# First chunk's v loaded as fp32 and cast on the engines, two of its loads moved behind weight pieces, first expert steps moved ahead

## Chip, cores and metric

The kernel runs on one core of a Trainium2 chip. The metric is the device time in microseconds (us) of one execution; the smaller, the better. Compute engines named below are PE (matrix multiply), DVE (vector), ACT (activation) and POOL (GpSimd); SP issues most transfers, POOL issues the others. All transfers share 16 DMA engines.

## What is computed

Two stages in a row. The first is a gated linear recurrence for 4 batches and 8 heads over 768 steps, with head size 48:

```python
f = 1.0 / (1.0 + np.exp(-f_logit))
for t in range(S):
    state = f[:, :, t, :, None] * state + np.einsum('bhd,bhe->bhde', k[:, :, t], v[:, :, t])
    y[:, :, t] = np.einsum('bhd,bhde->bhe', q[:, :, t], state)
```

The second takes the 3072 rows of 384 that come out and sums four expert networks, weighted by normalised probabilities:

```python
p = domain_probs / (domain_probs.sum(-1, keepdims=True) + 1e-09)
for e in range(E):                       # 4 experts, 384 -> 1024 -> 384
    out += p[:, e:e + 1] * (np.maximum(x @ w1[e], 0.0) @ w2[e])
```

## The kernel before

**Tiling.** The 768 steps are cut into six chunks of 128 (`c` = 0 to 5). Inside a chunk, each batch `b` has its recurrence turned into matrix products: `cs` and `cq` (L351, L362) sum the log gates on PE, `exps` and `expq` (L382, L387) turn the sums into factors on ACT, `q` and `k` (L394, L397) multiply q and k by the factors on DVE or POOL, `tpq` and `tpk` (L406) transpose the products on PE, `ev_tp` (L288) copies them out of PSUM, `at` (L437) makes the 128 x 128 scores, `ev_at0` and `ev_at1` (L449 on DVE, L445 on ACT) copy the two halves out, where the copy on ACT is masked afterwards by `mask1` on POOL (L441), and `y` (L464) multiplies them with `vb`, the bf16 values. `ev_y` copies y out, `xt` transposes it (L490) and `ev_xt` puts it where the experts read it. `kv` (L470) and `ev_kv` (L477) add the chunk to the carried state.

**Experts.** In chunk 0 the first expert's first layer goes batch by batch, in eight steps `h 0.0.fc.n` of 12 matmuls each (L499): `fc` 0 or 4 names the half of the hidden columns, `n` = 0, 128, 256, 384 the batch. From the second expert on a step `h` takes all four batches at once (3 matmuls of 512 columns), and steps `o` (L514) and `p` (L646, L654) make the second layer. `pp` (L324) transposes the probabilities.

**Names.** A number pair behind a step is chunk and batch: `y 0.1` is y of chunk 0, batch 1.

**Order.** A planner makes a list of steps with dependencies and a rank for each, taken in turn from the string `RANKS` at the top of the file. Every engine issues its steps in the order of these ranks, so an engine waits at its first step that isn't ready, and all that is behind waits with it. A letter behind a rank fixes the engine of the step: A is ACT, D is DVE, P is POOL. `FILLER` names steps in front of which PE runs matmuls of 512 columns whose result nobody reads (L1156).

**Transfers around the change.** SP issues the loads of f, k and q of chunk 0, then the probabilities. POOL issues, in the order of `SEQ` (L1170), the four loads of chunk 0's v and the eleven pieces of the weights, all on one queue. A transfer issued by POOL casts: the weights go from fp32 to bf16 on the way, and so do chunk 0's four v loads (L293), straight into the tiles `vb`. `w0` and `w1` are the two halves of expert 0's first layer. The first two v loads are held until the loads of k of batches 1 and 2 have landed (`GATE`). For later chunks v is loaded as fp32 by SP and cast by `cast_v` (L402).

**What follows chunk 0's loads.** f of chunk 1 comes in two halves. The second half (`ld f1.1`) is issued only once weight piece 8 has landed (L307). Its gate steps on ACT (L334, L342) stand in front of `cs 1.0` (L347), the first PE step of chunk 1's recurrence.

Of the kernel before, what the change touches and what calls it, by code (L numbers as in the profile page):

```python
# [77 lines left out]
FILLER = {"cs 0.0": 6, "tpk 0.1": 4}  # L78
# [65 lines left out]
def kernel(  # L144
# [11 lines left out]
    nc = tc.nc  # L156
# [1048 lines left out]
```

## Time and profile before

| what | us |
|---|---|
| median of 3 runs | 286.28 |
| the three runs | 286.17, 286.28, 289.65 |
| profiled execution, its time | 285.82 |
| profiled execution, span of its instructions | 284.1 |
| DVE, ACT, POOL busy | 208.7, 178.2, 185.3 |

The profile page lists for each engine its busy time and share of the span. PE is busy nearly throughout, and the others have a quarter to a third of the span free. An answer of the trace with a time line has the start, the length, the engine, the line of the code, what is written and read, and the count of instructions, with the engine's idle time before them and what ended it in brackets.

### The profile page before, as it was taken

What the parts mean: (1) busy time and instruction counts of PE and PEld (TensorE: products, weight loads), DVE (VectorE), ACT (ScalarE), POOL (GpSimd) and SP (SyncE); (2) the same over time, 40 slices, a digit from 0 to 9 for tenths busy, and PEclk for the clock granted to TensorE, in tenths of its full rate; (3) what the DMA queues carried; (4) which work ended last, traced back from release to release, by engine and by line L of the source; (5) the groups of instructions that cost most, each with busy time, mean ns of one, the idle gap of its engine ahead of it and who ended that gap; (6) DMA issues with size and microseconds to landing.
All of it is one profiled execution on the core that took longest, in us unless ns stands there. A gap on an engine that the chain in (4) does not pass through costs nothing.

```text
span 284.1 us, 8015 instructions
## 1 busy us (share of the span) xinstructions
PE 276.0 (97%) x3228; PEld 241.2 (85%) x3228; DVE 208.7 (73%) x437; ACT 178.2 (63%) x350; POOL 185.3 (65%) x197
## 2 busy tenths in 40 slices
PE   6889999999999999999999999999999999999995
PEld 4678565668788999999998999999999899999995
DVE  5695487797779587769887786686765687857683
ACT  5668235647898848686866867769367456556420
POOL 5799353706699878667729955695656545793761
PEclk9999999999999999999999999999999999999999
DMA  6999999999988999999999999996547015201003
GB/s 156 189 195 205 208 195 200 184 216 181 162 150 159 198 164 208 204 168 184 194 175 207 194 179 218 184 166 124 111 82 160 30 31 76 67 0 59 2 2 111
DMA packets 153688, 41.88 MB, mean 147 GB/s; under 512 B 144028, under 2 KB 152860, under 8 KB 153652
## 3 DMA queue, kind: packets, MB, share of 16 engines
q1 hardware_dynamic: 142404, 34.66, 65.1%
q0 software_dynamic: 11248, 6.72, 16.8%
q8 instruction: 25, 0.41, 0.6%
q14 instruction: 11, 0.09, 0.1%
HBM read 31.51 MB, written 4.72 MB: 128 GB/s over the span
## 4 chain that ended last, share of the span: by engine, by line
PE 84%; DMA 9%; POOL 4%; ACT 1%; DVE 1%; issue 0%; ACTq 0%; POOLq 0%
PE ps_m L646 29%; PE ps_m L531 26%; PE ps_m L574 7%; DMA w_sb<-in_moe_w_dram 7%; PE ps_m L514 6%; PE ps_m L499 4%; PE ps_m L654 2%; DMA f<-in_f_logit_dram 2%; PE ps_m L437 2%; POOL w_sb L312 2%; PE ps_m L464 1%; PE ps_m L460 1%; PE ps_m L347 1%; PE ps_m L470 1%; POOL AT L441 1%; PE ps_m L362 1%
## 5 line engine op out<-in xcount | busy, mean ns | idle before, releaser
L531 PE MATMUL ps_m<-x,w_sb 128*128 128x256 bf16 x672 | 84.3, 273 | 0.0
L531 PEld LDWEIGHTS <-w_sb 128*128 128x128 bf16 x672 | 63.6, 98 | 7.1
L595 ACT ACTIVATE h<-ps_m 128x512 bf16<-128x512 f32 x82 | 46.8, 600 | 24.1 <-PE ps_m L531 23.9
L646 PEld LDWEIGHTS <-S 128*128 128x128 bf16 x576 | 48.2, 98 | 0.8
L673 DVE TENSOR_TENSOR o<-ps_m,o 128x192 f32<-128x192 f32 x91 | 31.1, 353 | 19.1 <-PE ps_m L646 17.3
L646 PEld LDWEIGHTS <-h 128*128 128x128 bf16 x432 | 36.2, 98 | 0.8
L610 POOL TENSOR_TENSOR S<-h 128x1024 bf16<-128x1024 bf16 x14 | 29.7, 2124 | 10.3 <-DVE S L610 6.3
L499 PE MATMUL ps_m<-x,w_sb 128*128 128x128 bf16 (+2 forms) x264 | 35.1, 282 | 0.0
L420 ACT ACTIVATE yb<-ps_m,pn 128x384 bf16<-128x384 f32 x55 | 29.4, 586 | 8.5 <-PE ps_m L464 5.6
L397 POOL TENSOR_TENSOR qk<-q,e 128x384 bf16<-128x384 f32 x18 | 21.6, 1201 | 12.5 <-DVE f L549 3.9
L646 PE MATMUL ps_m<-ts_sb,S 128*128 128x192 bf16 x288 | 29.3, 246 | 0.0
L646 PE MATMUL ps_m<-w_sb,h 128*128 128x192 bf16 x288 | 29.2, 246 | 0.0
L646 PE MATMUL ps_m<-w_sb,S 128*128 128x192 bf16 x288 | 28.7, 246 | 0.0
L499 PEld LDWEIGHTS <-w_sb 128*128 128x128 bf16 x264 | 21.6, 98 | 8.1
L593 DVE TENSOR_SCALAR h<-ps_m 128x512 bf16<-128x512 f32 x30 | 20.6, 688 | 9.6 <-PE ps_m L531 8.5
L453 DVE TENSOR_TENSOR AT<-ps_m,mask 128x512 bf16<-128x512 f32 x40 | 25.6, 682 | 2.1 <-PE ps_m L437 2.0
L510 ACT ACTIVATE h<-ps_m 128x512 bf16<-128x512 f32 x33 | 19.1, 595 | 12.2 <-PE ps_m L499 11.8
L380 ACT ACTIVATE e<-ps_m 128x384 f32<-128x384 f32 x40 | 23.6, 708 | 3.2 <-PE ps_m L347 1.4
L610 POOL TENSOR_TENSOR S<-h,S 128x1024 bf16<-128x1024 bf16 x10 | 21.2, 2124 | 4.5 <-DVE o L673 2.5
L514 PE MATMUL ps_m<-w_sb,h 128*128 128x384 bf16 x128 | 23.9, 326 | 0.0
L585 DVE CUSTOM_DVE_ANT_0 h<-ps_m,QK 128x512 bf16<-128x512 f32 x24 | 16.0, 686 | 5.1 <-PE ps_m L574 1.9
L588 ACT COPY QK<-ps_m 128x512 f32<-128x512 f32 x24 | 13.8, 588 | 8.1 <-PE ps_m L574 5.2
(140 smaller groups left out, 523.3 us busy)
## 6 DMA issues: line engine op xcount, KB each, us to landing
out_dram<-o SPq DMA_DIRECT2D x23, 192.0 KB, 2.5
w_sb<-in_moe_w_dram POOLq DMA_DIRECT2D x5, 768.0 KB, 15.2
k<-in_k_dram SPq DMA_DIRECT2D x10, 384.0 KB, 5.1
q<-in_q_dram SPq DMA_DIRECT2D x10, 384.0 KB, 5.0
v<-in_v_dram SPq DMA_DIRECT2D x10, 384.0 KB, 5.1
f<-in_f_logit_dram SPq DMA_DIRECT2D x9, 384.0 KB, 5.8
w_sb<-in_moe_w_dram POOLq DMA_DIRECT2D x6, 384.0 KB, 8.2
f<-in_f_logit_dram SPq DMA_DIRECT2D x6, 192.0 KB, 4.4
```

Of the source, the lines that this page charges most:

```text
L380: nc.scalar.activation(out=o, in_=i, func=AF.Exp, scale=1.0 if j else -1.0)
L397: return engines[eng].tensor_tensor(out=tl("qk", c, b)[:, j, :, 0:D].rearrange("t (i r) d -> t i r d", r=2), in0=tl("qk"[j], c, b // 2)[:, ...
L420: nc.scalar.activation(out=ys, in_=y, func=AF.Copy, scale=pe)
L453: nc.vector.tensor_tensor(out=tl("AT", c, b)[:, r].rearrange("s i t -> s (i t)"), in0=tl("A", c, b, r).rearrange("s i t -> s (i t)"), in1= ...
L499: nc.tensor.matmul(out=hp(c, e, fc, n0, n1, nf)[:, f], lhsT=w1_sb[:, e, kk, (fc + f) * 128:(fc + f + 1) * 128], rhs=tl("xT", c)[:, kk, n0: ...
L514: nc.tensor.matmul(out=tl("op", c, e, nt)[:, 0:Din], lhsT=tl("h", c, e, half_of(c, nt * T))[:, fc, nt * T:(nt + 1) * T], rhs=w2_sb[:, e, f ...
L531: nc.tensor.matmul(out=out_[:, f], lhsT=w1_sb[:, e, kk, (fc + f) * 128:(fc + f + 1) * 128], rhs=tl("xs", c, hf, p)[:, el, kk, :], start=(k ...
L593: nc.vector.tensor_relu(out=dst, in_=tl("hp", c, hf, p, el, fc))
L595: nc.scalar.activation(out=dst, in_=tl("hp", c, hf, p, el, fc), func=AF.Relu)
L610: return engines[eng].tensor_tensor(out=o, in0=in0, in1=in1, op=op)
L646: nc.tensor.matmul(out=out_, lhsT=lhs[:, f, :], rhs=rhs[:, f, :], start=(first and el == 0 and f == 0), stop=(el == 1 and f == KH - 1), sk ...
L673: nc.vector.tensor_tensor(out=o, in0=src, in1=o, op=ALU.add)
```

## The change

Chunk 0's four v loads no longer cast. They go as fp32 into the tiles `v`, as in the later chunks, and a step `v 0.b` casts each into `vb`: `v 0.0` on DVE, `v 0.1`, `v 0.2` and `v 0.3` on ACT. In POOL's queue the third v load comes behind weight piece 0, the fourth behind weight piece 1. The ranks are new, and two fillers are added.

```diff
-FILLER = {"cs 0.0": 6, "tpk 0.1": 4}
+FILLER = {"cs 0.0": 6, "tpk 0.1": 4, "at 0.2": 2, "h 0.0.0.0": 3}
...
         if (c, nm) == (0, "v"):
-            ins[c, nm, b] = nc.gpsimd.dma_start(out=tl("vb", c, b), in_=srcs[nm][c, :, b * H:(b + n) * H, :])
+            ins[c, nm, b] = nc.gpsimd.dma_start(out=tl("v", c, b // 2)[:, hh(b, n), :], in_=srcs[nm][c, :, b * H:(b + n) * H, :])
...
             issued.append(P.add(f"v issue {i}", {"POOL": 0.8}, lambda _, i=i: load(0, "v", i, 1), -600 + 2 * j,
-                                deps=issued[-1:] + gate(x), takes=[("vb", 0, i)], lag=1.2))
-            ld[0, "v", i] = P.add(f"ld v0.{i}", {"DMA": 1.45}, lambda _: None, VW[0] + j, deps=issued[-1:] + fifo[-1:], lag=2.0)
+                                deps=issued[-1:] + gate(x), takes=[("v", 0, i // 2)], lag=1.2))
+            ld[0, "v", i] = P.add(f"ld v0.{i}", {"DMA": 1.0}, lambda _: None, VW[0] + j, deps=issued[-1:] + fifo[-1:], lag=2.0)
...
-            vb = ld[0, "v", b] if c == 0 else P.add(f"v {c}.{b}", {"POOL": 0.52, "ACT": 0.54}, one(cast_v), s(4),
+            vb = P.add(f"v {c}.{b}", {"POOL": 0.52, "ACT": 0.54} if c else {"POOL": 0.52, "ACT": 0.54, "DVE": 0.34}, one(cast_v), s(4),
                        deps=[ld[c, "v", b]], takes=[("vb", c, b)], frees=[("v", c, half)])
...
-SEQ = "v0 v1 v2 w0 v3 w1"
+SEQ = "v0 v1 w0 v2 w1 v3"
```

The new ranks (both strings are left out) leave the order of each engine as it was, but for these places, all in the first tenth of the program:

| engine | order before | order after |
|---|---|---|
| PE | at 0.2, xt 0.0, y 0.1, tpk 0.3, tpq 0.3, pp, kv 0.1, h 0.0.0.0, xt 0.1, at 0.3, y 0.2, kv 0.2, h 0.0.0.128, xt 0.2, h 0.0.4.0, y 0.3, h 0.0.4.128 | 2 fillers, at 0.2, xt 0.0, y 0.1, tpk 0.3, 3 fillers, h 0.0.0.0, tpq 0.3, xt 0.1, kv 0.1, pp, h 0.0.0.128, at 0.3, y 0.2, kv 0.2, h 0.0.4.0, xt 0.2, h 0.0.4.128, y 0.3 |
| DVE | ev_at1 0.0, ev_at0 0.1, ev_tp 0.2, k 0.3, q 0.3, ev_kv 0.0, ev_at0 0.2, ev_tp 0.3, ev_kv 0.1, ev_xt 0.1 | ev_at1 0.0, v 0.0, ev_at0 0.1, ev_tp 0.2, k 0.3, ev_kv 0.0, ev_at0 0.2, q 0.3, ev_xt 0.1, ev_tp 0.3, ev_kv 0.1 |
| ACT | ev_y 0.0, ev_at1 0.2, ev_xt 0.0, ev_y 0.1, ev_tp 0.3, relu 0.0.0.0, ev_y 0.2, relu 0.0.0.128, ev_xt 0.2 | ev_y 0.0, v 0.1, ev_at1 0.2, ev_xt 0.0, ev_y 0.1, ev_tp 0.3, v 0.2, relu 0.0.0.0, ev_y 0.2, v 0.3, relu 0.0.0.128, ev_xt 0.2 |
| POOL | issue of v0, v1, v2, w0, v3, then k 0.2, issue of w1, w2, then mask1 0.1, issue of w3, w4, w5, then mask1 0.2 | issue of v0, v1, w0, v2, then k 0.2, issue of w1, then mask1 0.1, issue of v3, w2, w3, w4, then mask1 0.2, issue of w5 |
| SP | loads of f0.3, k0.3, q0.3, then the probabilities | the probabilities, then f0.3, k0.3, q0.3 |

122 rows, old and new, of the table RANKS are left out of this document.

## The prediction

> **What bounds the kernel now.** I read the page first, then what PE waited for after its first expert step, then the chain that ended last.
>
> ```profile
> span 284.1 us, 8015 instructions
> PE 276.0 (97%) x3228; PEld 241.2 (85%) x3228; DVE 208.7 (73%) x437; ACT 178.2 (63%) x350; POOL 185.3 (65%) x197
> ```
>
> ```profile
> PE ps_m L347 <- ACT gp L342: 0.7, 1, 0.7
> ```
>
> The second fence is the whole answer for PE's waits from 18.9 us to the end: one. From there on PE works without a break, but for that wait at `cs 1.0`. So the change, which lies ahead of 26 us, can act in two ways only: through the time at which PE has got through the start, and through the time at which this one wait ends. The time line of PE around the wait, and the chain that leads to it:
>
> ```profile
> 47.51 0.81 PE L499 MATMUL ps_m<-x,w_sb 128*128 128x512 bf16 x3
> 49.01 0.48 PE L347 MATMUL ps_m<-gp,Ub 128*128 128x384 bf16 x2 [0.68 <-ACT gp L342]
> ```
>
> ```profile
> 22.65 18.79 DMA w_sb<-in_moe_w_dram
> 41.45 5.70 DMA f<-in_f_logit_dram
> 47.24 0.85 ACT f L334
> 48.11 0.85 ACT gp L342
> ...
> 50.81 1.94 PE ps_m L499 x9
> ```
>
> `cs 1.0` waits for the gate steps, these for `ld f1.1`, this for weight piece 8, and that for everything ahead of it in POOL's queue, the four v loads among it. PE's step before it began at 47.51 and holds PE for 0.65 (three matmuls of 512 columns; the last row has nine of them in 1.94), so PE was ready at 48.16 and started at 49.01: **0.85 us of slack**. Call D the delay of PE's stream at that place and X the time by which weight piece 8 lands earlier. Then `cs 1.0` starts at the later of 48.16 + D and 49.01 - X, and since PE doesn't wait afterwards, the whole time moves by the larger of D - 0.85 and -X. A start that costs PE nothing is worth 0.85 us at most.
>
> **X: the loads.** Bytes read stay, bytes written double, the cast goes. The DMA view for 10.5 to 14 us (both queues at work), and for 48 to 51 us, where SP's fp32 loads run alone in rows of 192 bytes, as v will be:
>
> ```profile
> q0 software_dynamic: 1754, 0.17, 91.2%
> q1 hardware_dynamic: 1464, 0.35, 67.3%
> ```
>
> ```profile
> q1 hardware_dynamic: 3620, 0.69, 115.6%
> ```
>
> Columns are packets, MB, and packet time as a share of 16 engines. A cast packet took 0.912 x 3.5 x 16 / 1754 = 29.1 ns, an fp32 packet 1.156 x 3 x 16 / 3620 = 15.3 ns. Packets overlap, so I go by the pace: q0's share of the packet time is 91.2 / 158.5, hence 2.01 us for 1754 packets, 1.18 us for the 1024 of one v load; alone, fp32 makes 1024 in 3 x 1024 / 3620 = 0.85 us. Four loads save 4 x 0.33 = **1.3 us**. The upper bound is by packet times, 4 x 1024 x (29.1 - 15.3) / 16 = 3.5 us; the lower is nothing, if POOL's queue moves an fp32 row no faster, or if the late issue of the fourth load leaves the queue empty for a moment. I take 1.3, the nearest row for the new shape; all that matters is whether it is over 0.6 (below).
>
> The Trainium skill, "DMA: Bandwidth & Descriptors", Specifications, speaks against it: transfers under 512 B are not at line rate because the engine reads, modifies and writes. Both shapes are under 512 B, so by that rule alone X could be 0 and the sum would be 286.3. The two packet times above differ, so I follow the rows.
>
> **D: the start of PE's stream.** PE, POOL, DVE and ACT before:
>
> ```profile
> 15.97 0.40 PE L437 MATMUL ps_m<-QK 48*128 48x128 bf16 x8 [0.53 <-DVE QK L288]
> 16.30 0.34 PE L490 MATMUL ps_m<-ident,yb 128*128 128x128 bf16 x3
> 16.48 0.19 PE L464 MATMUL ps_m<-vb,AT 128*128 128x48 bf16 x1
> 17.39 0.35 PE L464 MATMUL ps_m<-vb,AT 128*128 128x48 bf16 x7 [0.72 <-POOL AT L441]
> 17.58 0.61 PE L406 MATMUL ps_m<-ident,qk 128*128 128x128 bf16 x8
> 18.12 0.66 PE L324 MATMUL ps_m<-ident,o 24*128 24x24 f32 x4
> 18.71 0.34 PE L470 MATMUL ps_m<-vb,qk 128*128 128x96 bf16 x4
> 18.89 0.83 PE L499 MATMUL ps_m<-x,w_sb 128*128 128x128 bf16 x12
> ```
>
> ```profile
> 13.97 1.57 POOL L312 DMA_DIRECT2D w_sb<-in_moe_w_dram  x2
> 15.55 1.78 POOL L441 TENSOR_SCALAR_AFFINE_SELECT AT<-AT 128x512 bf16<-128x512 bf16 x1
> 19.60 0.65 POOL L441 TENSOR_SCALAR_AFFINE_SELECT AT<-AT 128x512 bf16<-128x512 bf16 x1
> ```
>
> ```profile
> 15.24 0.67 DVE L288 COPY QK<-ps_m 112x1024 bf16<-112x1024 bf16 x1
> 15.83 0.55 DVE L397 TENSOR_TENSOR qk<-k,e 128x384 bf16<-128x384 f32 x1
> 16.29 0.56 DVE L394 TENSOR_TENSOR qk<-q,e 128x384 bf16<-128x384 f32 x1
> 19.93 0.36 DVE L288 COPY x<-ps_m 128x384 bf16<-128x384 bf16 x1
> ```
>
> ```profile
> 13.99 0.75 ACT L445 CAST AT<-ps_m 128x512 bf16<-128x512 f32 x1
> 15.38 0.52 ACT L287 CAST yb<-ps_m 128x384 bf16<-128x384 f32 x1
> 16.44 0.73 ACT L445 CAST AT<-ps_m 128x512 bf16<-128x512 f32 x1 [0.54 <-PE ps_m L437]
> 17.03 0.48 ACT L287 COPY x<-ps_m 128x384 bf16<-128x384 bf16 x1
> 19.76 0.60 ACT L510 ACTIVATE h<-ps_m 128x512 bf16<-128x512 f32 x1 [0.49 <-PE ps_m L499]
> ```
>
> ```profile
> 10.05 1.11 SPq L320 DMA_DIRECT2D o<-in_moe_domain_probs_dram  x1
> ```
>
> PE lost 0.53 at `at 0.2`, waiting for DVE's `ev_tp 0.2`, and 0.72 inside `y 0.1`, waiting for `mask1 0.1` on POOL.
>
> *Cast of v 0.0 on DVE.* It stands in front of `ev_tp 0.2`, and DVE has no idle time there. No row has this cast on DVE. The nearest, by size and output, is the copy of 384 elements, 0.36; the fp32 product of the same size, 0.56, is the ceiling; the floor is half the copy, 0.18. I take 0.35. `at 0.2` moves from 15.97 to 16.32. The 2 fillers run in that wait (2 x 0.22, now 0.53 + 0.35 long): nothing. Without the wait they would cost 0.43.
>
> *Mask.* `mask1 0.1` comes one issue earlier. POOL is free of w1 at 13.97 + 1.57 / 2 = 14.75, and the half that it masks is copied by ACT until 13.99 + 0.75 = 14.74. On SP the probabilities, 1.11 to issue, now stand ahead of f0.3. What of that shows in f0.3's landing, no row tells; with all of it `ev_tp 0.2` would be 0.4 later still, with none nothing. I take half, which delays this copy to 15.3 and nothing else. The mask took 1.78 once and 0.65 once; the long one ran beside the two DVE products at 15.83 and 16.29, whose 0.55 + 0.56 is just the excess of 1.13. In the new order those come after 16.1 (`k 0.3`) and after 17.5 (`q 0.3`), so I take 0.65: done at 16.0, with 1.78 at 17.1. The Trainium skill has the mechanism, "GPSIMD Engine Reference", Key points: GpSimd shares its SBUF interfaces with VectorE and contends with instructions there that have two SBUF inputs. The two rows agree. By the rule `y 0.1` no longer waits for the mask; if the rule were not the cause, the mask would end at 17.1, `y 0.1` would be 0.2 later and the sum 285.9.
>
> *y 0.1 and the cast v 0.1.* `at 0.2` 16.32, `xt 0.0` 0.33 later at 16.65, `y 0.1` at 16.83 if `vb` is there. v1 was issued and landed so:
>
> ```profile
> L293 POOL DMA_DIRECT2D vb<-in_v_dram x1: 897/897/897, 8.9 to 8.9; - x1
> DMA to landing us min/median/max: 7.4/7.4/7.4
> ```
>
> It landed at 16.3. Unchanged, ACT casts it from 16.35 to 16.9 (0.52, as `ev_y 0.0`, the cast of the same size), in the 0.54 that ACT idled ahead of `ev_at1 0.2`. So `y 0.1` starts at 16.9, takes 0.19 (17.39 to 17.58), `tpk 0.3` some 0.25 (eight transposes had 0.54): PE is through at 17.34. The 3 fillers last 3 x 0.215 = 0.65, to 17.99.
>
> *h 0.0.0.0* needs `ev_xt 0.0`: `ev_at1 0.2` follows `at 0.2` at 16.78, `ev_xt 0.0` 0.59 later at 17.37, done at 17.85. And it needs w0, which was issued behind v2 and landed so:
>
> ```profile
> L312 POOL DMA_DIRECT2D w_sb<-in_moe_w_dram x1: 768/768/768, 10.7 to 10.7; - x1
> DMA to landing us min/median/max: 8.0/8.0/8.0
> ```
>
> That is 18.7; now v2 with 0.85 or more is behind it: 17.8 or earlier. So the step starts at 17.99, right behind the fillers, which are hidden but for 0.1; if `ev_xt 0.0` were early, all 0.65 would be PE's. Before, it started at 18.89, with `tpq 0.3`, `pp` and `kv 0.1` done, which PE now has still ahead: 0.27 (the other half of the 0.54), 0.59 (18.12 to 18.71) and 0.18 (18.71 to 18.89), together 1.04. D is 17.99 + 1.04 - 18.89 = **+0.14**.
>
> *Rest.* `v 0.2` falls into ACT's idle 0.49 ahead of the first relu (19.76). `v 0.3` stands ahead of `ev_xt 0.2`, which lets `h 0.0.0.256` in: between 0 and its 0.52; I take 0.1, as PE has `h 0.0.4.128` and `y 0.3` to do meanwhile. w1, moved ahead of v3, lands earlier than its step needs it. `q 0.3`, moved later on DVE, is needed only behind `h 0.0.0.0`.
>
> D = +0.25, X = 1.3: the time moves by the larger of 0.25 - 0.85 = **-0.6** and -1.3. The profiled execution took 285.82, 1.7 more than its span; it would take 285.2. The median of the runs, 286.28, becomes **285.7**.
>
> **Rivals.** *No gain:* X is near nothing, piece 8 lands when it did, `cs 1.0` starts at 49.01, and D up to 0.85 is swallowed there: 286.3. For it: the 15.3 ns are SP's queue, not POOL's, and SP's loads beside the cast took 0.673 x 3.5 x 16 / 1464 = 25.7 ns a packet. Against: the cast packets write half as much and still took longest. The rule of the Trainium skill on small transfers, above, would give this case.
>
> *Slower:* ACT stands at `v 0.1` for v1's landing, with `ev_at1 0.2`, `ev_xt 0.0` and `h 0.0.0.0` queued behind. A landing at t puts `h 0.0.0.0` at t + 1.6 (0.05 to start, the cast's 0.45 to the next start, 0.59 between 16.44 and 17.03, 0.48, 0.03), so D = 0.25 + t + 1.6 - 17.99. At 16.3 that is no loss yet, each further us costs one, and the slack of 0.85 is gone at t = 17.0. At 17.5, in the middle between v1's landing and w0's old one, D is 1.36: 286.28 + 0.51 = 286.8; at 18.7, with D at 2.56, it is 288.0. For it: v1 took 7.4 us to land, and its packets double in bytes. Against: nothing new is ahead of it in the queue but v0, and that gets no slower by any row.
>
> **How the numbers follow.** Forecast 0.55, no gain 0.22, slower 0.18, anything else 0.05. The forecast's own range is D from -0.1 (285.3) to 0.65 (286.1). The profiled execution lies 0.46 under the median, so runs scatter by that; the low end is 285.3 - 0.4 = 284.9. Upwards the range takes in no gain and the slower case up to its middle and the scatter of 0.4 on top, 287.2. Beyond 2%, 5.7 us, which is about what a measurement of this kernel can tell from no change, no case reaches: the start would have to lose six times its slack, or gain what it hasn't got. I leave 0.02 for faster, 0.03 for slower, 0.95 within.
>
> **What would show it.** Right: no wait of PE for POOL at L464; L441's first row near 0.65; the wait at L347 under 0.4; weight piece 8 landed by 40.9. Wrong: piece 8 at 41.4 again (no gain), a wait of ACT for a v load ahead of its cast, over 0.6 us (slower), or PE idle in front of its first L499 step.

## The result, and the profile after

| | before | changed |
|---|---|---|
| median of 22 runs each | 286.51 us | 287.62 us |
| lowest and highest | 285.47, 289.65 | 286.24, 289.09 |
| ratio, 95% interval | | 1.0042 [1.0026, 1.0059] |
| profiled execution, its span | 285.82, 284.1 | 287.77, 286.1 |

The change costs 0.4%, some 1.1 us, where 0.6 us less was forecast. Within 2% that counts as no change, but the whole interval lies above 1. The two profiled executions lie 1.95 us apart, more than the medians: that of the kernel before is 0.69 under its median, that of the changed kernel 0.15 above. The page of the changed kernel, its span and PE's row:

```profile
span 286.1 us, 8025 instructions
PE 277.6 (97%) x3228; PEld 241.9 (85%) x3233; DVE 209.5 (73%) x438; ACT 179.2 (63%) x353; POOL 183.3 (64%) x197
```

PE is busy 1.6 us longer. (The change adds five matmuls, the fillers; that the trace has as many matmul records as before means that some have no record.) What PE waited for from 12 us to the end of the work, whole answer:

```profile
PE ps_m L351 <- ACT gp L339: 1.7, 1, 1.7
PE ps_m L437 <- DVE QK L288: 0.7, 2, 0.5
PE ps_m L1156 <- issue: 0.2, 1, 0.2
```

The wait at L347 is gone, and so is the one for POOL at L464. A new one stands at the top, ahead of the whole stretch that the prediction spoke of: L351 is `cs 0.3`, which sums the log gates of chunk 0's last batch. PE's time line around it (start, length, engine, line, operands, count; idle time before in brackets):

```profile
12.88 0.40 PE L437 MATMUL ps_m<-QK 48*128 48x128 bf16 x8 [0.20 <-DVE QK L288]
14.97 0.49 PE L351 MATMUL ps_m<-gp,Up 128*128 128x192 bf16 x4 [1.69 <-ACT gp L339]
...
16.78 0.63 PE L1156 MATMUL ps_m<-S 128*128 128x512 bf16 x1 [0.22 <-issue]
17.34 0.61 PE L437 MATMUL ps_m<-QK 48*128 48x128 bf16 x8
17.88 0.50 PE L490 MATMUL ps_m<-ident,yb 128*128 128x128 bf16 x3
...
18.92 1.20 PE L1156 MATMUL ps_m<-S 128*128 128x512 bf16 x3
19.96 0.83 PE L499 MATMUL ps_m<-x,w_sb 128*128 128x128 bf16 x12
```

`cs 0.3` starts at 14.97; before it was 13.93, with hardly a gap ahead of it. (Of the two fillers ahead of `at 0.2` one has no record; the 0.22 before the other is most likely its place.) `at 0.2` (L437) starts at 17.34 where 16.32 was forecast, the first expert step at 19.96 where 17.99 was. The step `cs 0.3` waits for ACT's gate steps, and these for a load:

```profile
13.84 0.52 ACT L334 ACTIVATE f<-f 128x384 f32<-128x384 f32 x1 [2.48 <-DMA f<-in_f_logit_dram]
14.40 0.52 ACT L339 ACTIVATE gp<-f 128x384 bf16<-128x384 f32 x1
```

ACT stands 2.48 us for f0.3, the load that the probabilities were moved ahead of. What SP issued in the changed kernel, and below it the same load before:

```profile
7.78 0.63 SPq L320 DMA_DIRECT2D o<-in_moe_domain_probs_dram  x1
8.46 0.61 SPq L299 DMA_DIRECT2D f<-in_f_logit_dram  x1
```

```profile
7.80 0.63 SPq L299 DMA_DIRECT2D f<-in_f_logit_dram  x1
```

f0.3 is issued 0.66 later and lands 1.05 later, at 13.82 instead of 12.77. k0.3 and q0.3 behind it lose more: 15.87 and 17.95 instead of 14.44 and 15.92. So it isn't the issue alone. The transfer engines between 10 and 11 us, before and then changed (packets, MB, packet time as a share of 16 engines; q1 is SP's queue, q0 POOL's):

```profile
q1 hardware_dynamic: 494, 0.18, 68.0%
q0 software_dynamic: 238, 0.02, 49.3%
```

```profile
q0 software_dynamic: 37, 0.14, 67.4%
q1 hardware_dynamic: 67, 0.03, 10.8%
```

As long as v was cast on the way, POOL's queue moved rows one by one, in packets of 96 bytes, and SP's queue got 494 packets through beside it. As fp32 its packets are 3840 or 4224 bytes, 20 or 22 rows of 192 bytes, and SP's queue got 67 packets through. It looks as if the large packets crowded the small ones out, but the other kernels of the next section contradict it. The kernel with both moves undone (the probabilities last again, POOL's order as before) has the fp32 loads too; the same microsecond there:

```profile
q1 hardware_dynamic: 488, 0.18, 67.1%
q0 software_dynamic: 32, 0.13, 38.8%
```

In all 13 profiled executions with the probabilities last, SP's queue has 419 to 820 packets in this microsecond, whether v is cast or not; in the seven with the probabilities first it has 64 to 156, and two of these cast (140 and 156). So it is the place of the probabilities that thins out SP's queue here, not the size of the packets beside it.

What POOL's queue does to SP's shows later. The changed kernel between 14 and 16 us, when k0.3 and q0.3 are on their way and `w0` runs beside them, in packets of 1024 bytes:

```profile
q0 software_dynamic: 290, 0.33, 87.6%
q1 hardware_dynamic: 319, 0.11, 31.6%
```

The two queues move nearly as many packets, but SP's carry a third as many bytes. The Trainium skill, "DMA: Bandwidth & Descriptors", Queues, rings and completion order, says that an engine takes turns between the queues and empties a whole packet before it turns to the next; these two counts agree with that.

The clock is the third thing. Windows of 5 us, the changed kernel (busy time and count of each engine; then the granted clock of PE, the DMA share, GB/s):

```profile
10.00:15.00 5.00, 2.56 (x43) 1.88 (x41) 4.44 (x8) 2.17 (x6) 3.22 (x4) 1.00 1.10 219
15.00:20.00 5.00, 4.78 (x56) 3.33 (x57) 2.94 (x6) 3.71 (x9) 4.37 (x7) 0.66 1.17 237
```

After the wait PE's clock was at half from 16.29 to 19.70. Most of its additional busy time is fillers that ran in this stretch: 0.63 at 16.78, and the three at 18.92 last 1.20 instead of 0.65. From `at 0.2` to the first expert step it is 19.96 - 17.34 = 2.62 us, 0.95 more than forecast. The Trainium skill, "TensorE: Matmul & The Clock Gate", Part 1, gives half rate after at least one idle window of some 3.4 us. Here the fall lasted 3.41 us, but the wait ahead of it was 1.69 only, and PE was busy for 1.72 of the 3.41 us ahead of the fall; by this trace less than an idle window is enough.

From there to the end, PE around `cs 1.0` (L347) in the changed kernel:

```profile
50.10 0.81 PE L499 MATMUL ps_m<-x,w_sb 128*128 128x512 bf16 x3
50.74 0.49 PE L347 MATMUL ps_m<-gp,Ub 128*128 128x384 bf16 x2
```

No wait is left, and `cs 1.0` starts 1.74 later than before. PE's first step with 512 columns, at which expert 1 begins, starts at 28.65 instead of 26.06. So D is 2.58 (from unrounded times), of which the slack of 0.85 swallowed its share: 2.58 - 0.85 = 1.73. The first step of L531 starts 1.81 later, the end comes 1.95 later.

### The profile page after: what moved, and what is told of

The parts are those of the page before. It is cut to its first block, busy times and chain, and to the rows that moved or that the text cites. A ratio compares the mean times of both kernels' runs of the same rounds, so it can differ in the third digit from the quotient of the medians.

```text
span 286.1 us, 8025 instructions
## 1 busy us (share of the span) xinstructions
PE 277.6 (97%) x3228; PEld 241.9 (85%) x3233; DVE 209.5 (73%) x438; ACT 179.2 (63%) x353; POOL 183.3 (64%) x197
## 3 DMA queue, kind: packets, MB, share of 16 engines
q0 software_dynamic: 7344, 7.11, 15.2%
## 4 chain that ended last, share of the span: by engine, by line
PE 93%; SPq 3%; DMA 2%; ACT 1%; issue 0%; DVE 0%; ACTq 0%
PE ps_m L646 29%; PE ps_m L531 26%; PE ps_m L499 11%; PE ps_m L514 7%; PE ps_m L574 7%; PE ps_m L654 3%; PE ps_m L437 2%; DMA f<-in_f_logit_dram 2%; PE ps_m L464 2%; SPq L299 2%; PE ps_m L470 1%; PE ps_m L460 1%; PE ps_m L347 1%; SPq L301 1%; PE ps_m L406 1%; PE ps_m L1156 1%
## 5 line engine op out<-in xcount | busy, mean ns | idle before, releaser
L531 PE MATMUL ps_m<-x,w_sb 128*128 128x256 bf16 x672 | 84.3, 273 | 0.0
L531 PEld LDWEIGHTS <-w_sb 128*128 128x128 bf16 x672 | 63.6, 98 | 7.1
L595 ACT ACTIVATE h<-ps_m 128x512 bf16<-128x512 f32 x82 | 46.8, 599 | 24.8 <-PE ps_m L531 24.6
L673 DVE TENSOR_TENSOR o<-ps_m,o 128x192 f32<-128x192 f32 x91 | 31.1, 353 | 18.8 <-PE ps_m L646 17.0
L588 ACT COPY QK<-ps_m 128x512 f32<-128x512 f32 x24 | 13.8, 588 | 8.1 <-PE ps_m L574 5.2
## 6 DMA issues: line engine op xcount, KB each, us to landing
w_sb<-in_moe_w_dram POOLq DMA_DIRECT2D x5, 768.0 KB, 14.9
```

The source lines that it names most:

```text
L531: nc.tensor.matmul(out=out_[:, f], lhsT=w1_sb[:, e, kk, (fc + f) * 128:(fc + f + 1) * 128], rhs=tl("xs", c, hf, p)[:, el, kk, :], start=(k ...
L595: nc.scalar.activation(out=dst, in_=tl("hp", c, hf, p, el, fc), func=AF.Relu)
L673: nc.vector.tensor_tensor(out=o, in0=src, in1=o, op=ALU.add)
```

## The experiments

Each kernel is timed in five rounds beside the kernel before on the same chip, but for two that are profiled once. An interval is about 0.2 to 0.3% to either side, so most of these kernels can't be told from each other by their times; what tells them apart is where their traces differ. The table has, of each profiled execution, the landing of f0.3, q0.3 and w0, the start of the first 512-column step, the landing of f1.2 and the span. (f of chunk 1 comes in three loads, f1.0 and f1.1 with one batch each and f1.2 with batches 2 and 3.)

| kernel | f0.3 | q0.3 | w0 | first 512 | f1.2 | span | ratio to before |
|---|---|---|---|---|---|---|---|
| before | 12.8 | 15.9 | 18.7 | 26.06 | 59.2 | 284.1 | |
| changed | 13.8 | 17.9 | 16.8 | 28.65 | 59.0 | 286.1 | 1.0042 [1.0026, 1.0059] |
| changed, again | 13.4 | 19.9 | 17.0 | 28.64 | 57.5 | 286.0 | 1.0040 [1.0016, 1.0065] |
| probabilities last | 12.6 | 17.6 | 16.8 | 26.50 | 59.5 | 284.5 | 1.0014 [0.9986, 1.0042] |
| before, probabilities first | 12.7 | 16.2 | 19.9 | 28.50 | 58.8 | 285.9 | 1.0002 [0.9970, 1.0034] |
| casting loads | 13.4 | 18.8 | 17.4 | 27.89 | 59.5 | 285.3 | 1.0030 [1.0006, 1.0054] |
| no new fillers | 13.0 | 18.1 | 17.3 | 27.16 | 58.0 | 284.5 | 1.0038 [1.0007, 1.0070] |
| POOL's order back | 13.2 | 18.7 | 18.0 | 27.96 | 59.7 | 285.4 | 1.0017 [0.9998, 1.0036] |
| fillers at cs 0.3 | 13.6 | 19.5 | 16.6 | 28.28 | 58.9 | 285.6 | 1.0024 [1.0003, 1.0045] |
| both back | 11.6 | 16.2 | 17.7 | 26.42 | 59.1 | 284.0 | 1.0025 [1.0004, 1.0047] |
| before, POOL's new order | 12.4 | 17.5 | 17.6 | 27.88 | 59.6 | 285.1 | 1.0016 [0.9987, 1.0046] |

### The probabilities alone

The changed kernel with the probabilities behind q0.3 on SP again:

```diff
     pl = P.add("ld p", {"DMA": 0.2}, lambda e: load_p(), -989.5, takes=[("o", "praw")], lag=3.0)
+    pl.prio = 58.5
```

> The changed kernel with the load of the probabilities put back behind q0.3 on SP, nothing else. In the changed kernel's profile f0.3 landed at 13.8 us (12.8 before), and PE stood 1.7 us at cs 0.3 for it. Theory V (the fp32 loads of v, whose rows travel in packets of 4 KB, crowd SP's small packets out between 10 and 11 us): f0.3 still lands at 13.4 or later, PE still waits 1.2 us or more at cs 0.3, and the ratio to the kernel before stays at 1.002 or more. Theory P (the probabilities issued ahead of f0.3 delay it): f0.3 lands by 13.1, the wait is under 0.9, and the ratio falls to 1.001 or less.

f0.3 landed at 12.65, `cs 0.3` started at 13.80 without a wait, D was 0.44 instead of 2.58, and `cs 1.0` started at 48.64, 0.37 earlier than in the kernel before. D was 0.97 in the one other execution with this start (with f1.1 let go earlier, below). So the place of the probabilities makes most of D in this kernel. But its end was 0.4 later than before, not 0.4 earlier, and its ratio, 1.0014, lies between what the two theories expected. The time lines of ACT and PE at 60 us show where the gain went:

```profile
59.51 0.84 ACT L334 ACTIVATE f<-f 128x768 f32<-128x768 f32 x1 [3.35 <-DMA f<-in_f_logit_dram]
60.26 0.46 ACT L287 CAST yb<-ps_m 128x384 bf16<-128x384 f32 x1
```

```profile
60.13 0.33 PE L470 MATMUL ps_m<-vb,qk 128*128 128x96 bf16 x4
60.78 0.34 PE L490 MATMUL ps_m<-ident,yb 128*128 128x128 bf16 x3 [0.32 <-ACT yb L287]
```

In the kernel before the same places read:

```profile
59.20 0.84 ACT L334 ACTIVATE f<-f 128x768 f32<-128x768 f32 x1 [2.67 <-DMA f<-in_f_logit_dram]
59.95 0.46 ACT L287 CAST yb<-ps_m 128x384 bf16<-128x384 f32 x1
```

```profile
60.49 0.33 PE L470 MATMUL ps_m<-vb,qk 128*128 128x96 bf16 x4
60.66 0.33 PE L490 MATMUL ps_m<-ident,yb 128*128 128x128 bf16 x3
```

ACT's gate step of f1.2 stands in front of `ev_y 1.0` (L287), which PE's `xt 1.0` (L490) needs. In both kernels ACT idles there for f1.2. Before, PE came to `xt 1.0` just when `ev_y 1.0` was done; with a stream that is 0.37 earlier it waits, and `xt 1.0` starts 0.12 later than before; 0.28 more are lost behind it. This is a second floor, and nothing in PE's waits of the kernel before names it, as PE lost nothing at it.

The other way round, the kernel before with only the probabilities moved ahead of f0.3:

```diff
     pl = P.add("ld p", {"DMA": 0.2}, lambda e: load_p(), -989.5, takes=[("o", "praw")], lag=3.0)
+    pl.prio = 26.5
```

> The kernel before with the load of the probabilities moved ahead of f0.3 on SP, nothing else: the casting loads of v stay. Theory P: f0.3 lands at 13.5 or later and PE waits over a microsecond at cs 0.3. Theory V: f0.3 lands by 13.2, and the time is that of the kernel before within 0.15%, since what is left is swallowed by the slack of 0.85 us at cs 1.0.

f0.3 was issued at 8.45, as late as in the changed kernel, and still landed at 12.73, and `cs 0.3` started at 13.88. The ratio is 1.0002. Taken alone, this reads as if the later issue cost nothing beside casting loads. But the landing of f0.3 scatters. It was 11.38 to 12.77, 12.17 in the mean, in the 13 profiled executions with the probabilities last, and 12.73 to 13.82, 13.29 in the mean, in the seven with them first; this one is the earliest of the seven. With the probabilities first f0.3 is issued 0.72 later and lands 1.1 later in the mean, and whether v is cast matters little: 13.0 against 12.1 where it is, 13.4 against 12.2 where it isn't. So this one execution doesn't show that the later issue costs nothing. It has a late w0 (19.90) besides, and a wait of PE for it, which isn't the probabilities' doing by this trace:

```profile
PE ps_m L499 <- DMA w_sb<-in_moe_w_dram: 1.5, 1, 1.5
```

Why w0 was late isn't shown; in the five other executions with casting loads and POOL's old order it landed at 18.6 to 19.7. Two of these, which differ from the kernel before only after 36 us (f1.1 let go earlier, below), had their first 512-column step at 27.98 and 29.55: PE waited for w0, and the clock fell to half. So the 26.06 against which D is counted is the best of three starts of this kernel.

### The fp32 loads, POOL's order, both

The changed kernel with the v loads casting again, into `vb`, and without the cast steps:

```diff
-            ins[c, nm, b] = nc.gpsimd.dma_start(out=tl("v", c, b // 2)[:, hh(b, n), :], in_=srcs[nm][c, :, b * H:(b + n) * H, :])
+            ins[c, nm, b] = nc.gpsimd.dma_start(out=tl("vb", c, b), in_=srcs[nm][c, :, b * H:(b + n) * H, :])
...
-            vb = P.add(f"v {c}.{b}", {"POOL": 0.52, "ACT": 0.54} if c else {"POOL": 0.52, "ACT": 0.54, "DVE": 0.34}, one(cast_v), s(4),
+            vb = P.add(f"v {c}.{b}" if c else f"no v {b}", {"POOL": 0.52, "ACT": 0.54} if c else {"POOL": 0.01, "ACT": 0.01, "DVE": 0.01}, one(cast_v) if c else (lambda e: None), s(4),
...
```

> The changed kernel with the four loads of v casting again, straight into vb, and without the four cast steps; order, ranks and fillers as changed. Theory V: f0.3 lands by 13.3, PE's wait at cs 0.3 is under 0.9 us, the clock stays at full, expert 1's first step starts by 26.8 us (28.6 in the changed kernel, 26.1 before), and the ratio is between 0.998 and 1.001. Theory P: f0.3 still lands at 13.5 or later and the ratio stays at 1.003 or more.

The ratio is 1.0030 [1.0006, 1.0054]: the loss stays without fp32 and without casts. f0.3 is late again (13.35), k0.3 later than in either execution of the changed kernel (17.54), q0.3 between the two (18.80). Neither theory has it in full: f0.3 landed between what the two expected, the wait at `cs 0.3` and the full clock are V's, the ratio is P's. PE's waits:

```profile
PE ps_m L406 <- DVE qk L397: 0.9, 1, 0.9
PE ps_m L351 <- ACT gp L339: 0.9, 1, 0.9
```

The wait is split between `cs 0.3` and `tpk 0.3`, which needs k0.3. So the large packets of the fp32 loads aren't what is needed for the loss, striking as they are; weight piece 0, moved ahead of the third v load, is the other new thing on the queue. POOL's order alone undone:

```diff
-SEQ = "v0 v1 w0 v2 w1 v3"
+SEQ = "v0 v1 v2 w0 v3 w1"
```

> The changed kernel with POOL's loads in the old sequence (v0 v1 v2 w0 v3 w1), all else as changed: fp32 loads, casts, probabilities first, new order on PE, fillers. Theory W (weight piece 0 ahead of v2 slows SP's last loads, since its 1 KB packets alternate with SP's small ones): q0.3 lands by 16.9 us instead of 17.9, k0.3 by 15.2 instead of 15.9, PE stands less at cs 0.3 and behind it, and the ratio to the kernel before falls to 1.002 or less, although w0 itself now lands about 0.8 us later. Theory P (the probabilities' place alone): nothing changes, 1.003 or more.

f0.3 landed at 13.16, q0.3 at 18.73, and `cs 0.3` waited 1.9; the landings that theory W expected (k0.3 by 15.2, q0.3 by 16.9) were missed. The ratio, 1.0017 [0.9998, 1.0036], is lower than the changed kernel's; the start was later than before all the same. Both undone together:

```diff
+    pl.prio = 58.5
...
-SEQ = "v0 v1 w0 v2 w1 v3"
+SEQ = "v0 v1 v2 w0 v3 w1"
```

> The changed kernel with the probabilities behind q0.3 on SP again and POOL's loads in the order v0 v1 v2 w0 v3 w1 again; fp32 loads, casts, fillers and the new order of PE stay. Theory Q (SP's last loads are late because of the probabilities and of w0 in front of v2, both): f0.3, k0.3 and q0.3 land as in the kernel before (12.8, 14.4, 15.9, each within 0.6), PE's first L499 step starts when w0 has landed, about 18.5 or later, ratio 1.000 to 1.002. Rival O (the new order of PE and the fillers cost the time themselves): cs 0.3 is at 13.9 and the first 512-column step of L499 is still at 27.5 or later, ratio 1.003 or more.

Here all three loads land as before or earlier (11.6, 14.4, 16.2), and D is 0.36, near the forecast 0.25. What is left of the start is a wait for w0, at PE's first expert step, which the new order reaches earlier than the weights:

```profile
PE ps_m L499 <- DMA w_sb<-in_moe_w_dram: 1.0, 1, 1.0
```

The span is 284.0, no longer than before, but the median of its 12 runs, 286.68, is 0.25% above the kernel before; the profiled execution, 285.72, is the second fastest of them. To see what it doesn't show, the same kernel was profiled twice more.

> The same kernel as with both undone, a second look. If PE's new order stands for w0: a wait at L499 of 1 us or more, longer where w0 lands after 17.7, and the span is longer by what that wait has over 1.0. If not: w0 has landed before PE is there and the span is near 284 all the same.

> The same kernel once more, a third look, with the same two readings: a wait at L499 for w0 of 1 us or more and a span longer by what it has over 1.0, or no wait there and a span near 284.

Neither reading holds in full. The waits for w0 were 0.3 and none, as PE came at about 17.8, when w0 landed. D was 0.43 and 0.59. The spans were 284.3 and 284.9; in both PE came to `xt 1.0` too early, where f1.2 landed at 59.43 and 60.01, and in the third execution it had stood for `cs 1.0` too (f1.1 landed at 47.36). So it isn't w0 that makes the difference between the three, but chunk 1's two loads of f.

POOL's order alone on the kernel before:

```diff
-SEQ = "v0 v1 v2 w0 v3 w1"
+SEQ = "v0 v1 w0 v2 w1 v3"
```

> The kernel before with POOL's order of the changed kernel (v0 v1 w0 v2 w1 v3) alone: casting loads, the probabilities last on SP, the old order of PE. Theory Q: SP's q0.3 lands later than 15.9 (17 or later), k 0.3 and q 0.3 follow, but w0 lands at about 17, so PE doesn't wait at its first L499 step; ratio 0.999 to 1.003. Rival O (only PE's new order costs, POOL's order costs nothing): q0.3 lands by 16.5, ratio 0.998 to 1.000.

q0.3 landed at 17.5, w0 at 17.6. PE was at `tpq 0.3` before `q 0.3` was done:

```profile
PE ps_m L406 <- DVE qk L394: 1.6, 2, 1.2
```

Over all 20 profiled executions q0.3 landed between 15.3 and 16.7 in ten of the eleven that had POOL's old order with the probabilities last or with casting loads, and at 18.1 in the eleventh. It landed between 17.5 and 19.9 in the nine that have w0 in front of the third v load, or fp32 loads and the probabilities first. So an earlier w0 is paid by SP's last loads, packet for packet as between 14 and 16 us above. In the old order of PE `tpq 0.3` stands ahead of the first expert step and suffers for it; the new order has it behind.

### Fillers and the clock

The changed kernel without the five new fillers:

```diff
-FILLER = {"cs 0.0": 6, "tpk 0.1": 4, "at 0.2": 2, "h 0.0.0.0": 3}
+FILLER = {"cs 0.0": 6, "tpk 0.1": 4}
```

> The changed kernel without its two new fillers (2 and 3 matmuls). Theory F (the five fillers lie on PE's path): the time falls by up to 5 x 0.216 = 1.1 us at full clock, ratio about 1.000. Theory V (PE waits there anyway): nothing is gained, ratio 1.003 or more, and more if PE's clock falls for longer.

The ratio stays at 1.0038 [1.0007, 1.0070]. D was 1.10 in its profiled execution, one of the faster ones (286.20, median 287.28), but the clock was at half from 14.65 to 18.07, and in 9 of its 12 runs the mean granted clock was below 0.9965 (one stretch of 3.41 us at half makes 0.994), where it was in 10 of 22 with the fillers. And six more fillers in the new wait, to keep the clock up:

```diff
-FILLER = {"cs 0.0": 6, "tpk 0.1": 4, "at 0.2": 2, "h 0.0.0.0": 3}
+FILLER = {"cs 0.0": 6, "tpk 0.1": 4, "at 0.2": 2, "h 0.0.0.0": 3, "cs 0.3": 6}
```

> The changed kernel with 6 more idle matmuls (1.3 us) in front of cs 0.3, inside the wait that its profile shows there. Theory C (PE's clock, which fell to half for 3.4 us behind that wait in the profiled execution, carries the loss): the granted clock stays at full and the time falls by 0.7 us or more against the changed kernel, ratio 1.002 or less. If the loss is the late loads alone: ratio 1.003 or more, clock full or not.

The clock stayed full in 11 of 12 runs. The window of 15 to 20 us and PE's waits:

```profile
15.00:20.00 5.00, 4.02 (x66) 2.94 (x64) 2.90 (x6) 3.46 (x9) 4.63 (x7) 1.00 1.18 235
```

```profile
PE ps_m L406 <- DVE qk L394: 1.2, 1, 1.2
```

D fell from 2.58 to 2.22 only, as PE now stood at `tpq 0.3` for q0.3 (landed 19.5). Here the half clock covered a wait that would have been there anyway; by this one execution it is the smaller part of D. The times can't say it: 1.0024 [1.0003, 1.0045] overlaps the changed kernel's interval.

### The slack, and the second floor

The kernel before with fillers in front of its first expert step, four in the first run, twelve in the second:

```diff
-FILLER = {"cs 0.0": 6, "tpk 0.1": 4}
+FILLER = {"cs 0.0": 6, "tpk 0.1": 4, "h 0.0.0.0": 4}
```

> The kernel before with 4 idle matmuls (4 x 0.216 = 0.86 us) in front of h 0.0.0.0, from where PE works without a break. If the slack of 0.85 us at cs 1.0 is real: the wait at L347 goes to nothing and the time doesn't move, ratio within 0.9985 to 1.0015. If a delay of the start counts in full: 1.003.

> The kernel before with 12 idle matmuls (2.59 us) in the same place, about the delay that the changed kernel's profile shows at expert 1's first step. With the slack: 2.59 - 0.85 = 1.74 us more, ratio 1.006. If a delay counts in full: 1.009.

Four measured 0.9994 [0.9972, 1.0016], no loss, as expected; but in the profiled execution they delayed nothing (the first 512-column step at 25.84), so this run doesn't measure the slack. It shows the second floor instead: f1.1 landed early (46.40), `cs 1.0` started at 48.25, 0.76 earlier than in the kernel before, PE waited 0.53 at `xt 1.0`, and the span is 284.1 as before. Twelve measured 1.0013 [0.9987, 1.0038], less than expected: their 2.59 us made the first 512-column step only 1.72 later, `cs 1.0` 0.87 and the end 0.85 later. 1.72 - 0.85 = 0.87: here the slack of 0.85 at L347, and that the end follows by the rest, are measured.

Then the first floor was lifted: f1.1 let go by weight piece 7 instead of 8, on the changed kernel with the probabilities last, on the kernel before, and on the changed kernel with both undone:

```diff
-    w_last, w_gate = len(pieces) - 1, len(pieces) - 3
+    w_last, w_gate = len(pieces) - 1, len(pieces) - 4
```

> The changed kernel with the probabilities behind q0.3 again, and the second half of chunk 1's f (ld f1.1) let go when weight piece 7 has landed, not piece 8. Theory F (after the start, the landing of f1.1 and then of f1.2 on SP hold PE back at L347 and at L490 behind ev_y 1.0; a start that is earlier is given back there): f1.1 lands 3 us or more earlier, f1.2 earlier too, no gap of PE at 60 us, L531 0.4 to 0.9 earlier than 89.30 of the kernel before, ratio 0.996 to 0.9995. Rival C (the earlier loads of chunk 1 collide with weight pieces 8 and 9, which then land later, and PE waits for them): a wait of PE at L499 or L514 for weights or a later f1.2, ratio 1.001 or more.

> The kernel before with ld f1.1 let go when weight piece 7 has landed. Theory F: the wait at L347 (0.7) goes, cs 1.0 starts at 48.2, and as f1.2 lands earlier too, most of the 0.85 us stays to the end: ratio 0.997 to 0.9985. If only L347 is lifted and f1.2 still comes at 59.2, the ratio is 0.999 to 1.000 and PE has a gap near 60 us. Rival C: 1.001 or more.

> The changed kernel with the probabilities last again, POOL's order of the kernel before again, and ld f1.1 let go with weight piece 7. If PE's new order waits for w0 at its first L499 step, it does so here too: a wait of 1 us or more there, ratio 1.001 to 1.003. If the order costs nothing and only f1.1 and f1.2 held the gain back: ratio 0.997 to 0.999.

They measured 0.9996 [0.9971, 1.0021], 1.0013 [0.9996, 1.0031] and 1.0039 [1.0012, 1.0066]: no gain. f1.1 was issued 4 to 5 us earlier, at 36.7 to 37.1, but landed at 46.8 in the first two and 47.3 in the third, against 47.15 before; weight pieces 8 and 9 were now on their way beside it. The third shows the second floor best. ACT and PE:

```profile
60.47 0.84 ACT L334 ACTIVATE f<-f 128x768 f32<-128x768 f32 x1 [3.77 <-DMA f<-in_f_logit_dram]
```

```profile
61.73 0.34 PE L490 MATMUL ps_m<-ident,yb 128*128 128x128 bf16 x3 [0.74 <-ACT yb L287]
```

f1.2 landed at 60.44, `xt 1.0` started 1.29 later, and the span was 285.3. Wherever PE came to `xt 1.0` too early, these 1.29 us come again: 59.49 and 60.78 (probabilities last), 59.31 and 60.60 (four fillers), 59.43 and 60.72, 60.01 and 61.30 (both back, second and third execution). From `xt 1.0` to the end it is 223.5 to 223.7 us in all of them, and in the kernel before, without a wait, 284.1 - 60.66 = 223.4. There, f1.2 landed at 59.18, so the floor was 60.47, only 0.19 us ahead of PE.

A last pair held chunk 2's first load until weight piece 10 had landed, to free the engines for f1.2; the earlier f1.1 is in both, the first is otherwise the kernel before, the second has both moves undone:

```diff
         if (c, nm, b) == (1, "f", 1):
             after(ins[c, nm, b], ins["w", w_gate])
+        if (c, nm, b) == (2, "f", 0):
+            after(ins[c, nm, b], ins["w", 10])
```

> The kernel before with ld f1.1 let go with weight piece 7, and the load of chunk 2's first f held until weight piece 10 has landed. Theory F (two floors, f1.1 at L347 and f1.2 at L490): no wait at L347, f1.2 landed by 58, no gap of PE at 60 us, L531 0.5 to 0.9 earlier relative to PE's start than in the kernel before, ratio 0.997 to 0.999. If f1.2's landing isn't moved by the later load, or if chunk 2's q and k now come late: ratio 1.000 or more, with a PE wait after 60 us.

> The changed kernel with the probabilities last, POOL's old order, f1.1 let go with weight piece 7 and chunk 2's first f held until weight piece 10 has landed; it differs from the run with both undone and the earlier f1.1 (1.0039) by the last part alone. Theory F: f1.2 lands 1 us or more earlier than 60.44, no gap of PE at L490 near 61 us, ratio 0.998 to 1.001. If f1.2's landing is no floor: the gap goes elsewhere, ratio 1.003 or more as without it.

They measured 1.0022 [0.9990, 1.0055] and 1.0016 [0.9990, 1.0042]. f1.2 landed at 59.05 and 59.76, about as ever, and PE stood at `xt 1.0` in the second; so this didn't lift the floor, and whether a gain follows once it is lifted stays open. In the first, PE stood for w0, which landed at 19.66, for 1.9 us, and the clock was at half for 6.83 us from 19.11 on.

Last, the changed kernel once more beside three of the others:

> The changed kernel as it is, beside the three others on one chip. Ratio to before 1.003 to 1.006, f0.3 landed at 13.0 to 13.9, first 512-column step of L499 at 27.5 to 28.7 by theory Q; if the first comparison was an accident of one chip, 1.001 or less.

1.0040 [1.0016, 1.0065], the first 512-column step at 28.64 where it had been 28.65: the loss isn't an accident of one chip.

## Why the prediction was wrong

**The frame held for losses.** The time moved by D - 0.85 once D was over 0.85: 1.73 by this against 1.74 at `cs 1.0` and 1.95 at the end, and 0.87 against 0.85 with twelve fillers.

**D was the step that failed**: 2.58 us, not 0.25. The prediction said of the probabilities in front of f0.3: "What of that shows in f0.3's landing, no row tells; [...] I take half, which delays this copy to 15.3 and nothing else." Two things were wrong in it. First, f0.3 also feeds the gate steps of `cs 0.3`, on PE itself, and in the kernel before PE had next to no slack there (the gate steps ended at 13.87, `cs 0.3` started at 13.93); a later f0.3 is a later PE, and it comes before the wait at `at 0.2` in which the prediction looked for cover. Second, the size: half of 1.11 was taken from the length of the issue. The issue turned out at 0.63 here, but f0.3 landed 1.05 later in these two executions and 1.1 later in the mean of seven against 13; all of the 1.11, which the prediction named and halved, would have come close, though by luck, as the issue itself was shorter. Why a later issue of 0.7 makes a later landing of 1.1 isn't shown. q0.3 landed 2.03 later; `w0` ahead of the third v load has a part in that. Nor did the sum have a term for the clock. By the prediction's own milestones: `at 0.2` was 1.02 later than forecast, from there to the first expert step it took 0.95 more at half clock, and from this step to expert 1 it took 19.96 to 28.65, 8.69, against 7.17 before and 1.14 more forecast (1.04 and the 0.1 of the *Rest*), so another 0.38. 0.25 + 1.02 + 0.95 + 0.38 = 2.60. Neither rival named this place: the slower one had ACT wait for a v load, and v1 landed at 14.25, two us earlier than before. It is the same mechanism at another load of another queue.

**X was 0.4 in the two profiled executions, not 1.3.** Weight piece 8 landed at 41.06 instead of 41.44. Over the traces, it landed at 41.04 in the mean of the twelve with fp32 loads and at 41.43 in the mean of the eight that cast, with single ones from 40.3 to 42.0, so that the scatter of one execution is as large as the difference. The packet time of SP's queue was the wrong row, since POOL's queue packs some twenty fp32 rows together. The loads did get faster: v1 landed at 14.2 to 14.8 in the twelve, at 14.9 to 16.3 in the eight. The low bound, nothing, was closer than the value taken, and so was the rule of the Trainium skill, "DMA: Bandwidth & Descriptors", Specifications, that transfers under 512 B aren't at line rate, by which X could be 0. Why loads that land earlier at 14 us leave so little at 41 us isn't shown.

**"PE doesn't wait afterwards" was true only at the old speed.** The forecast of -0.6 needed all that lies behind `cs 1.0` to have as much slack. At `xt 1.0` there were 0.19 us. With D at 0.44 the probabilities-last kernel won 0.37 us at `cs 1.0` and gave back 0.49 by `xt 1.0`. So even with D as forecast, this change could have gained 0.2 us at most while f1.2 landed where it did.

**What was right**: the mask, no longer beside the two DVE products, took 0.63 and 0.65 us, and PE no longer waited for POOL at L464 (this agrees with the Trainium skill, "GPSIMD Engine Reference", Key points, on the shared SBUF interfaces); the cast of v 0.0 on DVE took 0.34; the wait at L347 went, but by luck, because PE came late. In two variants the mask did meet q's product on DVE, which took 0.55 where it ran alone in the changed kernel: the product took 0.99 and the mask 0.63 with POOL's order back, 0.83 and 1.00 without the new fillers. So either of the two can be the one that is held up.

**What stays open**: the kernel with both moves undone has three profiled executions of 285.7, 286.0 and 286.6 and a median of 286.68 beside 285.78 for the kernel before. D and f1.2 explain the three, not the median. So of the 0.40% that the changed kernel lost on the same chip, 0.25% stays with both moves undone, and how much of the loss in the medians is D's isn't shown; the fp32 loads, the casts, the new order of PE and the fillers are left as rivals. Nor can the times, with their intervals, say which of the two moves costs more. None of the variants beat the kernel before: the lowest ratios, 0.9994 (four fillers) and 0.9996 (probabilities last, f1.1 earlier), have intervals around 1.

## What to carry to other kernels

Of a load that is moved, follow every consumer, the ones on the bounding engine first, and ask for each whether the engine has slack at that step; a row that shows no wait shows no slack either. A queue's loads can be late because of what another queue carries, so a reordering on one is also a reordering on the others. And before a gain is counted, look at the engines beside the bound: a load for which a helper engine idles for microseconds is a floor that the bound has not reached yet. Last, the difference between two profiled executions is not the difference between the kernels: it was 1.95 us here and 1.11 between the medians, as loads and the clock move from run to run.

## What was unexpected in the hardware

POOL's queue moves fp32 rows of 192 bytes 20 or 22 at a time, in packets of 3840 or 4224 bytes, where it moved casting rows one by one in packets of 96. Beside weights in packets of 1024 bytes SP's queue got one packet for each of them, 319 to 290, and so a quarter of the bytes. PE's clock fell to half for 3.41 us after waits of 1.2 to 1.7 us (1.69, 1.52 and 1.17 in three of these kernels; PE was busy for 1.72, 1.89 and 1.99 of the 3.41 us ahead of the fall), and not in every run: in 10 of 22 of the changed kernel. And the same load of the same kernel moves from run to run: q0.3 landed at 17.9 in one execution of the changed kernel and at 19.9 in another, with the same end to 0.1 us.
